# Where VectorE takes its block sums in the first groups of a fused attention and mixer kernel

## The chip, the cores and the metric

The kernel runs on one core of a Trainium2 chip. Its time is the device time of one execution in microseconds (us), and less is better. The core has five engines, each with an instruction queue of its own that it works off in order: TensorE (PE in the profile, its weight loads PEld), VectorE (DVE), ScalarE (ACT), GpSimd (POOL) and SyncE (SP, which here only issues DMAs). They wait for each other through semaphores.

## The reference

```python
xn = _layernorm(x)                                   # 2048 x 512
q  = (xn @ wq).reshape(B, Sq, 32, 128)               # 32 heads of 128
p  = softmax(einsum("bhqd,bhkd->bhqk", q, k_cache) * 128 ** -0.5)
s  = einsum("bhqk,bhkd->bhqd", p, v_cache) ... @ wo  # heads side by side, 4096 -> 512
# g = silu(block_B(xn)): layernorm, w1, gelu, shifts, w2, residual, layernorm, w3, gelu, w4, residual
return x + s * g
```

## The kernel before, in words

Ahead of the attention stands a prologue of some 120 us: layer norms, the mixer block B, and the gates, which go to DRAM. What follows is attention, cut into 128 **units**. Unit u is one head for 512 queries; the order is group g of four heads (8 of them), then query tile qt (4), then head hh in the group (4), so a group has 16 units and units 0 to 15 are group 0 (`units`, line 126). Every unit has eight **slots** p = 0 to 7, and n = 8u + p counts them all. The loop at line 1131 writes out, slot by slot, what each engine is given; nothing reorders it afterwards (`pin` keeps program order). In a slot PE gets two score matmuls (`s_slot`, `ps_s`), two matmuls of probabilities with V for the slot ten slots earlier (`pv_slot`, `ps_o`), and between them small products. ACT takes the exponentials of a slot into a tile `pT` (line 446); two slots share one tile, so a unit has four.

Two kinds of small products lie between those matmuls, and both use a scheme with seven block products where a plain one has eight. The scheme needs sums and differences of blocks, which VectorE makes beforehand.

- **Queries.** From unit 14 on, q for two heads at a time is made from blocks of `xnT` and of `wq`. `x_sum(qt, i)` (lines 355 to 367, run at line 366) makes four sums of each query tile, once for all; number 2 overwrites a block of `xnT` in place, except for tile 3. `w_sum(h, i)` (369 to 376, run at line 375) makes four differences for each pair of heads. `product` issues the matmuls (`ps_q`), and `q_part` (lines 423 to 431) adds them together on VectorE. The last of these, line 431, writes the `qT` that the next unit's score matmuls read. Before unit 14, q comes from plain matmuls, copied out by `q_copy` (line 341).
- **Output projection.** `wo_sum(g, i)` (lines 553 to 563, run at line 562) makes four differences of the group's `wo`; number 2 is made in place in groups 0 to 5, in group 6 in the second buffer of `tw0`. `o_sum` (line 571) makes the sums of the attention output `oT`, each in a single buffer `so0` to `so3`, and `wo_product` issues the matmuls into `ps_wo`. They all use one PSUM tile, tag `xm`, and VectorE's `wo_take` (line 596) adds its halves to the accumulator `sacc` before PE may write there again. The first four token tiles of group 0 use plain matmuls, copied by line 655.

For the softmax denominators VectorE adds the four `pT` tiles of a unit into `acc`: `add_first` (line 452) at slot 4 adds the first two, then the third follows (line 461, or in two halves at line 457: one half by GpSimd from slot 6 of the unit, the other by VectorE early in the next one) and the fourth (line 461). `fold` and `fold_last` (465, 469) halve the result twice. SP transposes it by DMA (`tT`, line 494), VectorE reduces it in the unit after (499, 505), SP sends the reciprocals to DRAM and back to all partitions (`rb`, lines 507 and 511), and the product at line 523 normalizes `ps_o`.

What decides where a sum stands is written out by hand: the list of units in line 1120 for `x_sum` (four for tile 3, then tiles 0, 1 and 2, each at the end of slot 3 of its unit), line 1123 for `w_sum` (slot 4), line 1084 for `wo_sum` (offsets in slots around the group's unit 6, for group 0 unit 10), and `APART` in line 1056 for the units whose third `pT` tile is added in two halves. The tile pool `qt` (line 89) gives `qT` tiles of 1 KB a partition, six in turn.

Of the kernel before, what the change touches and what calls it, by code (L numbers as in the profile page):

```python
# [11 lines left out]
BF16 = mybir.dt.bfloat16  # L12
# [5 lines left out]
def kernel(  # L18
# [16 lines left out]
    P = nc.NUM_PARTITIONS  # L35
# [3 lines left out]
    Sq, D = x2d.shape  # L39
# [11 lines left out]
    HG = 4  # L51
    NG = H // HG
# [11 lines left out]
    def pool(name, bufs=1, space=None, **kw):  # L64
        if space is not None:
            kw["space"] = space
        return tc.tile_pool(name=name, bufs=bufs, **kw)
# [21 lines left out]
    qtp = ent(pool("qt", 6))  # L89
# [11 lines left out]
    pR = right.enter_context(pool("pR", side="right", reuse_waits="tile"))  # L101
# [9 lines left out]
    def mm(out, lhsT, rhs, start, stop, **kw):  # L111
# [9 lines left out]
        out=ident[:], in0=diag[:], scalar1=0.0, scalar2=None, op0=ALU.is_equal))  # L121

    HEAD = 7
    XS = 3 * QT + 1
    TW = (2, 1, 0, 1)
# [3 lines left out]
    NU = len(units)  # L129
# [5 lines left out]
    def at(n, fn):  # L135
        todo[n].append(fn)
# [194 lines left out]
               xnT[:, dc, qt * 512:(qt + 1) * 512], dc == 0, dc == DC - 1)  # L331

    def q_copy(u, eng=None):
        pl, tag = (pR, "qR") if u < HEAD else (qtp, "qT")
        qT = pl.tile([P, 512], BF16, tag=tag, **(dict(bufs=HEAD) if u < HEAD else {}), name="qT")
        src, dst = st[u].pop("psq")[:], qT[:]
        if u in TURN:
            src = src.rearrange("d (r j) -> d j r", j=4)
            dst = dst.rearrange("d (j r) -> d j r", j=4)
        if eng is None:  # L340
            pin(nc.vector.tensor_copy(out=dst, in_=src))
        else:
            pin(nc.scalar.activation(out=dst, in_=src, func=ACT.Identity))
        st[u]["qT"] = qT[:]
# [10 lines left out]
    def x_sum(qt, i):  # L355
        if i == 2 and qt < QT - 1:
            out = x_block(qt, 1, LO)
        else:
            out = pS.tile([P, 2, 256], BF16, tag="xs", bufs=XS, name="xs")[:]
        a, b, op = (  # L360
            (x_block(qt, 1, LO), x_block(qt, 1, HI), ALU.add),
            (xs.get((qt, 0)), x_block(qt, 0, LO), ALU.subtract),
            (x_block(qt, 0, LO), x_block(qt, 1, LO), ALU.subtract),
            (x_block(qt, 0, HI), xs.get((qt, 1)), ALU.subtract),
        )[i]
        pin(nc.vector.tensor_tensor(out=out, in0=a, in1=b, op=op))
        xs[qt, i] = out
# [87 lines left out]
    def add_half(u, eng, part):  # L455
        a, e = st[u]["acc"], st[u]["pT"][2]
        pin(eng.tensor_tensor(out=a[:, part, :], in0=a[:, part, :], in1=e[:, part, :], op=ALU.add))  # L457

    def add_next(u, i):
        a = st[u]["acc"]  # L460
        pin(nc.vector.tensor_tensor(out=a[:], in0=a[:], in1=st[u]["pT"][i][:], op=ALU.add))  # L461
# [91 lines left out]
    def wo_sum(g, i):  # L553
        w = wog[g]
        b11, b12, b21, b22 = (w[:, k, c] for k in (UP, DOWN) for c in (WL, WR))
        if i == 2 and g < NG - 2:
            out = b12
        else:
            j = 0 if i == 2 else i
            out = pS.tile([P, 2, D // 2], BF16, tag=f"tw{j}", bufs=TW[j], name="tw")[:]  # L560
        a, b = ((b12, b11), (b22, tw.get((g, 0))), (b22, b12), (b21, tw.get((g, 1))))[i]
        pin(nc.vector.tensor_tensor(out=out, in0=a, in1=b, op=ALU.subtract))
        tw[g, i] = out
# [46 lines left out]
    wog, sp, tw, so, wo_ps, gin = {}, {}, {}, {}, {}, {}  # L610
# [36 lines left out]
    def pay():  # L647
        while owed:
            y_out(*owed.popleft(), nc.sync)
# [181 lines left out]
    def q_ahead(u):  # L831
        q_mm(u, range(DC), ("xa", "xm")[len(made) % 2])
        q_copy(u, nc.scalar)
        made.append(u)
# [155 lines left out]
    pS = None  # L990
    for h in range(HG):
        load_wo(h)
    for g in range(NG - 1):
        b = (g * QT + QT - 1) * HG
        for hh in range(HG):
            h = (g + 1) * HG + hh
# [56 lines left out]

    FIRST, LAST = 14, NU - 4
    BLOCK = [(g, qt) for g in range(NG - 1) for qt in range(QT)][1:-2]
    APART = range(2 * HG + 1, NU - 3)
    pairs = range(FIRST, LAST + 1, 2)
    q_plan = defaultdict(list)
    steps = defaultdict(list)
# [21 lines left out]
            which[u0 + n].append((o_sum, g, qt, i))  # L1081
    for g in range(NG - 1):
        u0 = ((g * QT + (g == 0)) * HG + 6) * SPU
        for i, n in ((0, -4), (2, -4 if 0 < g < NG - 2 else 4), (1, 4), (3, 12)):
            o_early[u0 + n].append((wo_sum, g, i))
    for i, (qt, u) in enumerate((qt, qt * HG + 5 + j) for qt in range(1, QT) for j in range(2)):
        at(u * SPU + 6, lambda qt=qt, i=i: sa_clear(qt, i % 2))
# [3 lines left out]
    for i, u in enumerate((10, 11, 12, 13, 14, 16, 18, 20)):  # L1091
        n = (LATER + u) * SPU
# [10 lines left out]
    def add_last(u):  # L1103
        if u in APART:
            add_half(u, nc.vector, HI)
        add_next(u, 3)
# [10 lines left out]
        for fn, *args in plan.get(n, ()):  # L1117
            fn(*args)

    for j, u in enumerate((9, 9, 9, 9, 12, 12, 13, 13, 13, 16, 17, 17, 18, 19, 20, 20)):  # L1120
        at(u * SPU + 3, lambda qt=(j // 4 - 1) % QT, i=j % 4: x_sum(qt, i))
    for h in range(2, H, 2):
        for i, u in enumerate((((-4, -3, -3, -3), (-1, -1, 0, 0))[h % HG // 2] if h >= HG else (11,) * 4)):
            o_early[(h // HG * QT * HG + u) * SPU + 4].append((w_sum, h, i))

    for v in range(1, NU):
# [4 lines left out]
    for n in range(UB * SPU):  # L1131
        u, p = divmod(n, SPU)
# [33 lines left out]
        for v, k in ((u + 1, 3), (u + 2, 7)):  # L1166
            if p == k and "psq" in st.get(v, ()) and (k == 3) == (v > FIRST):
                q_copy(v)
# [31 lines left out]
        if p == 6:  # L1200
            add_half(u, nc.gpsimd, LO) if u in APART else add_next(u, 2)
        pay()
# [3 lines left out]
        if pS is None and not held:  # L1206
            right.close()
            pS = right.enter_context(pool("pS", side="right", reuse_waits="tile"))
# [3 lines left out]
    n = UB * SPU  # L1212
# [27 lines left out]
    def pv_to(k):  # L1240
# [29 lines left out]
        out=diag[:], in0=diag[:], scalar1=0.0, scalar2=None, op0=ALU.is_equal))  # L1270
# [98 lines left out]
```

## Time and profile before

| | |
|---|---|
| median of three timed runs | 1224.51 us (1224.1 to 1224.75) |
| the profiled execution: its own time | 1222.83 us |
| its span, first to last instruction | 1221.1 us |
| granted TensorE clock | 1.000 |
| PE, ACT, DVE, POOL busy, share of the span | 99%, 91%, 89%, 24% |

The profile is one execution on the chip. Its page gives busy times, the chain of work that ended last and the costliest groups of instructions. The timeline gives single instructions of one engine: start and duration in us, engine, line of the kernel, operation, output<-inputs with their shapes, and in brackets the idle time of the engine before it with what ended it. Rows of equal instructions that follow each other are merged (x2). Matmuls are pipelined: a matmul of 512 columns is listed with 0.38 us, and two of them with 0.59, but the next one starts 0.216 us after it, so a pair takes 0.43; pairs of 256 columns take 0.22. VectorE's instructions overlap by some hundredths of a microsecond in the same way. The view of windows gives the busy time of each engine in a stretch.

### The profile page before, as it was taken

Reading aid. Unit: us, or ns where it says so; the run is one execution under the profiler, and the core shown is the slowest. Engines: PE = TensorE matmul, PEld = TensorE weight load, DVE = VectorE, ACT = ScalarE, POOL = GpSimd, SP = SyncE. Lnnn points to the kernel's source line nnn. Section 1 sums busy time; section 2 is a strip of 40 time slices with the busy share of each in tenths; the row PEclk is TensorE's granted clock in tenths of the full one; section 3 lists DMA queues with packets and bytes.
Section 4 is the critical chain, followed back from the end, with each engine's and each line's share of the span. In section 5 each row is a group of like instructions: output and inputs, shape, how many; then the busy total and the mean of one; then the engine's idle time right before and its main releaser. Section 6 shows DMA issues by size and latency. Waiting matters only on the chain.

```text
span 1221.1 us, 18821 instructions
## 1 busy us (share of the span) xinstructions
PE 1208.6 (99%) x6534; PEld 673.7 (55%) x6657; DVE 1089.9 (89%) x1931; ACT 1107.6 (91%) x1243; POOL 297.6 (24%) x221
## 2 busy tenths in 40 slices
PE   9999999999999999999999999999999999999998
PEld 6466444555555555555555555555555555555555
DVE  7863778999999999999999899999999999989997
ACT  6345999999999999999999999999999999999996
POOL 5300001233222222222222222222222222223320
PEclk9999999999999999999999999999999999999999
DMA  7662323434343434344344433444433534455552
GB/s 178 169 153 59 56 57 83 96 85 98 75 90 88 99 66 90 85 99 88 70 95 84 103 69 83 92 96 78 87 83 91 100 66 90 87 101 110 124 113 66
DMA packets 248159, 113.07 MB, mean 93 GB/s; under 512 B 195328, under 2 KB 231296, under 8 KB 248064
## 3 DMA queue, kind: packets, MB, share of 16 engines
q1 hardware_dynamic: 244560, 107.21, 40.9%
q0 software_dynamic: 2944, 4.20, 1.5%
q8 instruction: 52, 0.85, 0.3%
q14 instruction: 43, 0.35, 0.2%
q10 hardware_dynamic: 560, 0.46, 0.1%
HBM read 69.60 MB, written 4.45 MB: 61 GB/s over the span
## 4 chain that ended last, share of the span: by engine, by line
PE 92%; DVE 5%; issue 1%; DMA 1%; ACT 1%; SPq 0%; DVEq 0%; POOL 0%; ACTq 0%
PE ps_s L112 39%; PE ps_o L112 35%; PE ps_q L112 8%; PE ps_wo L112 8%; PE ps_m L112 3%; DVE acc L461 1%; DVE acc L452 1%; DVE sacc L596 1%; ACT pT L446 1%; DMA kT<-in_A_k_cache_dram 0%; DVE acc L457 0%; DVE sm L499 0%; DMA tT<-acc 0%; DMA xin<-in_A_x_dram 0%; PE ps_oh L112 0%
## 5 line engine op out<-in xcount | busy, mean ns | idle before, releaser
L446 ACT ACTIVATE pT<-ps_s 128x1024 bf16<-128x1024 f32 x1016 | 1016.6, 1028 | 44.5 <-PE ps_s L112 13.0
L112 PE MATMUL ps_s<-qT,kT 128*128 128x512 bf16 (+1 forms) x2056 | 607.5, 377 | 0.8 <-ACT pT L446 0.4
L112 PE MATMUL ps_o<-pT,vb 128*128 128x512 bf16 x1884 | 568.3, 379 | 4.7
L457 POOL TENSOR_TENSOR acc<-acc,pT 128x1024 bf16<-128x1024 bf16 x116 | 246.8, 2128 | 727.4 <-DVE acc L452 395.6
L112 PEld LDWEIGHTS <-vb 128*128 128x128 bf16 x1984 | 194.0, 98 | 216.5
L112 PEld LDWEIGHTS <-kT 128*128 128x128 bf16 x2064 | 231.0, 113 | 72.4 <-DVE qT L431 1.4
L461 DVE TENSOR_TENSOR acc<-acc,pT 128x2048 bf16<-128x2048 bf16 x138 | 168.9, 1224 | 21.5 <-ACT pT L446 5.5
L452 DVE TENSOR_TENSOR acc<-pT 128x2048 bf16<-128x2048 bf16 x127 | 154.7, 1218 | 11.2 <-ACT pT L446 11.1
L596 DVE TENSOR_TENSOR sacc<-ps_wo,sacc 128x512 f32<-128x512 f32 x200 | 121.6, 608 | 3.4 <-PE ps_wo L112 2.4
L523 DVE TENSOR_TENSOR oT<-ps_o,rb 128x512 bf16<-128x512 f32 x127 | 86.5, 681 | 6.6 <-DMA rb<-dr 5.9
L465 DVE TENSOR_TENSOR acc<-acc 128x1024 bf16<-128x1024 bf16 x127 | 87.3, 687 | 2.4
L499 DVE TENSOR_REDUCE sm<-tT 128x4 f32<-128x512 bf16 x124 | 83.9, 676 | 6.0 <-DMA tT<-acc 5.4
L457 DVE TENSOR_TENSOR acc<-acc,pT 128x1024 bf16<-128x1024 bf16 x116 | 79.6, 686 | 0.0
L112 PEld LDWEIGHTS <-wc 128*128 128x128 bf16 x448 | 43.8, 98 | 52.9
L112 PE MATMUL ps_wo<-wo_h,oT 128*128 128x256 bf16 (+1 forms) x294 | 70.7, 307 | 0.5
L112 PEld LDWEIGHTS <-oT 128*128 128x128 bf16 x428 | 41.6, 98 | 45.6
L112 PEld LDWEIGHTS <-so 128*128 128x128 bf16 x400 | 39.1, 98 | 48.4 <-issue 1.7
L112 PEld LDWEIGHTS <-wq_h 128*128 128x128 bf16 x396 | 38.7, 98 | 46.0
L112 PE MATMUL ps_q<-xnT,wq_h 128*128 128x256 bf16 (+1 forms) x281 | 58.2, 294 | 0.2
L301 ACT ACTIVATE h2T<-ps_s 128x1024 bf16<-128x1024 f32 x28 | 28.7, 1023 | 31.6 <-PE ps_s L112 31.6
L469 DVE TENSOR_TENSOR acc<-acc 128x512 bf16<-128x512 bf16 x127 | 53.4, 420 | 2.4
L112 PEld LDWEIGHTS <-w_sb 128*128 128x128 bf16 x368 | 33.5, 98 | 29.2
(134 smaller groups left out, 924.4 us busy)
## 6 DMA issues: line engine op xcount, KB each, us to landing
rb<-dr SPq DMA_DIRECT2D x127, 256.0 KB, 3.8
vb<-in_A_v_cache_dram SPq DMA_DIRECT2D x62, 256.0 KB, 3.0
wq_h<-in_A_wq_dram SPq DMA_DIRECT2D x32, 128.0 KB, 2.5
wo_h<-in_A_wo_dram SPq DMA_DIRECT2D x32, 128.0 KB, 2.3
w_sb<-in_B_w_dram SPq DMA_DIRECT2D x8, 256.0 KB, 4.6
kT<-in_A_k_cache_dram SPq DMA_TRANSPOSE x128, 2.6
gate<-xall POOLq DMA_DIRECT2D x16, 128.0 KB, 2.3
sacc<-in_A_x_dram POOLq DMA_DIRECT2D x8, 256.0 KB, 4.6
```

Of the source, the lines that this page charges most:

```text
L112: pin(nc.tensor.matmul(out=out, lhsT=lhsT, rhs=rhs, start=start, stop=stop, **kw))
L301: pin(nc.scalar.activation(out=h2[c][:, f], in_=ps[:], func=ACT.Gelu_apprx_tanh))
L446: pin(nc.scalar.activation(out=s["pT"][-1][:, jj:jj + 2, :], in_=sps[:], func=ACT.Exp, scale=SCALE))
L452: pin(nc.vector.tensor_tensor(out=s["acc"][:], in0=s["pT"][0][:], in1=s["pT"][1][:], op=ALU.add))
L457: pin(eng.tensor_tensor(out=a[:, part, :], in0=a[:, part, :], in1=e[:, part, :], op=ALU.add))
L461: pin(nc.vector.tensor_tensor(out=a[:], in0=a[:], in1=st[u]["pT"][i][:], op=ALU.add))
L465: pin(nc.vector.tensor_tensor(out=a[:, 0:2, :], in0=a[:, 0:2, :], in1=a[:, 2:4, :], op=ALU.add))
L469: pin(nc.vector.tensor_tensor(out=a[:, 0, :], in0=a[:, 0, :], in1=a[:, 1, :], op=ALU.add))
L499: pin(nc.vector.tensor_reduce(out=sm[:], in_=s["tT"][:], axis=mybir.AxisListType.X, op=ALU.add))
L523: pin(nc.vector.tensor_tensor(out=to, in0=o, in1=rb, op=ALU.mult))
L596: pin(nc.vector.tensor_tensor(out=out, in0=ps, in1=out, op=ALU.add))
```

## The change

VectorE and GpSimd get the same sums at other places:

- `x_sum`: eight sums move. Tile 3: from unit 9 (four) to units 8, 8, 9, 9. Tile 0: from 12, 12, 13, 13 to 9, 9, 9, 11. Tile 1: from 13, 16 to 11, 13, and its last two stay in 17. Tile 2 stays in 18 to 20.
- `w_sum` of heads 2 and 3: from unit 11 (four) to units 8, 8, 9, 9.
- Unit 8's third `pT` tile is added in two halves, one by GpSimd; before, this began with unit 9.
- `wo_sum` number 2 of group 6: from slot 4 of unit 102 to slot 4 of unit 101, that is eight slots or one unit ahead of where it stood. It now has a tile of the pool `qt` instead of the second buffer of `tw0`. For that the pool's ring of `qT` has five tiles instead of six, and the last unit's `qT` a tile of its own.

The order of instructions on PE, ACT and SP is the same in both kernels.

```diff
     def q_copy(u, eng=None):
-        pl, tag = (pR, "qR") if u < HEAD else (qtp, "qT")
-        qT = pl.tile([P, 512], BF16, tag=tag, **(dict(bufs=HEAD) if u < HEAD else {}), name="qT")
+        pl, tag, n = (pR, "qR", HEAD) if u < HEAD else (qtp, "qT", 5) if u < NU - 1 else (qtp, "qL", 1)
+        qT = pl.tile([P, 512], BF16, tag=tag, bufs=n, name="qT")
...
         if i == 2 and g < NG - 2:
             out = b12
+        elif i == 2:
+            out = qtp.tile([P, 2, D // 2], BF16, tag="qT", bufs=5, name="tw")[:]
         else:
-            j = 0 if i == 2 else i
-            out = pS.tile([P, 2, D // 2], BF16, tag=f"tw{j}", bufs=TW[j], name="tw")[:]
+            out = pS.tile([P, 2, D // 2], BF16, tag=f"tw{i}", bufs=TW[i], name="tw")[:]
...
-    APART = range(2 * HG + 1, NU - 3)
+    APART = range(2 * HG, NU - 3)
...
-        for i, n in ((0, -4), (2, -4 if 0 < g < NG - 2 else 4), (1, 4), (3, 12)):
+        for i, n in ((0, -4), (2, -4 if g else 4), (1, 4), (3, 12)):
...
-    for j, u in enumerate((9, 9, 9, 9, 12, 12, 13, 13, 13, 16, 17, 17, 18, 19, 20, 20)):
+    for j, u in enumerate((8, 8, 9, 9, 9, 9, 9, 11, 11, 13, 17, 17, 18, 19, 20, 20)):
         at(u * SPU + 3, lambda qt=(j // 4 - 1) % QT, i=j % 4: x_sum(qt, i))
     for h in range(2, H, 2):
-        for i, u in enumerate((((-4, -3, -3, -3), (-1, -1, 0, 0))[h % HG // 2] if h >= HG else (11,) * 4)):
+        for i, u in enumerate((((-4, -3, -3, -3), (-1, -1, 0, 0))[h % HG // 2] if h >= HG else (8, 8, 9, 9))):
```

## The prediction

> **What bounds the kernel now.** I read the page first, then the windows, then PE's timeline in the stretches where it idles.
>
> ```profile
> PE 1208.6 (99%) x6534; PEld 673.7 (55%) x6657; DVE 1089.9 (89%) x1931; ACT 1107.6 (91%) x1243; POOL 297.6 (24%) x221
> PE 92%; DVE 5%; issue 1%; DMA 1%; ACT 1%; SPq 0%; DVEq 0%; POOL 0%; ACTq 0%
> ```
>
> PE is busy nearly all of the span, and its instructions stay what they are and in their order. So the change can win only time in which PE stands still. The second row says where to look: VectorE holds 5% of the chain that ended last, in a few stretches where PE came to wait for it. The view of windows, with one row for each stretch, gives the ceiling (PE's busy time is the second figure):
>
> ```profile
> 196.00:270.00 74.00, 72.61 (x368) 38.49 (x374) 70.18 (x130) 68.75 (x75) 21.41 (x12) 1.00 0.45 93
> 980.00:1000.00 20.00, 19.78 (x107) 10.99 (x108) 19.00 (x35) 19.05 (x22) 4.25 (x2) 1.00 0.32 58
> ```
>
> From 196 to 270 us (units 8 to 16, where the moved sums stand) PE idles 1.39 us, and 0.22 from 980 to 1000 (units 101 and 102): 1.6 us in all.
>
> PE's timeline shows the places, and VectorE's the instruction that ended each:
>
> ```profile
> 232.72 0.59 PE L112 MATMUL ps_o<-pT,vb 128*128 128x512 bf16 x2
> 233.78 0.38 PE L112 MATMUL ps_wo<-wo_h,so 128*128 128x256 bf16 x2 [0.47 <-DVE sacc L596]
> ...
> 242.43 0.38 PE L112 MATMUL ps_wo<-tw,oT 128*128 128x256 bf16 x2
> 243.25 0.62 PE L112 MATMUL ps_s<-qT,kT 128*128 128x512 bf16 x2 [0.44 <-ACT pT L446]
> ...
> 267.72 0.59 PE L112 MATMUL ps_o<-pT,vb 128*128 128x512 bf16 x2
> 268.43 0.38 PE L112 MATMUL ps_wo<-wo_h,so 128*128 128x256 bf16 x2
> ```
>
> ```profile
> 233.05 0.68 DVE L596 TENSOR_TENSOR sacc<-ps_wo,sacc 128x512 f32<-128x512 f32 x1
> 242.51 0.68 DVE L431 TENSOR_TENSOR qT<-ps_q,tq 128x512 bf16<-128x512 f32 x1
> 267.70 0.68 DVE L596 TENSOR_TENSOR sacc<-ps_wo,sacc 128x512 f32<-128x512 f32 x1
> ```
>
> A pair of 512 columns takes 0.43 and a pair of 256 takes 0.22, so from start to start PE loses 233.78 - 232.72 - 0.43 = **0.63 us**, 243.25 - 242.43 - 0.22 = **0.60** and 268.43 - 267.72 - 0.43 = **0.28**: 1.51 together (idle time by the records is less, since a record runs 0.16 past the next start). Each time PE starts again 0.05 us after VectorE's row ends (233.73, 243.19, 268.38). The second is put down to ACT, but that exponential ended with it by chance: the matmul reads the `qT` that line 431 had just written. So VectorE is up to 0.6 us late at three points, and each stall carries over: VectorE works without a pause, PE waits for it.
>
> **The change part by part.** Prices and the free room come from VectorE's rows of units 8 to 10, one of PE and one of GpSimd:
>
> ```profile
> 195.72 1.21 DVE L452 TENSOR_TENSOR acc<-pT 128x2048 bf16<-128x2048 bf16 x1
> ...
> 198.15 1.23 DVE L461 TENSOR_TENSOR acc<-acc,pT 128x2048 bf16<-128x2048 bf16 x1 [0.41 <-ACT pT L446]
> 199.29 0.69 DVE L655 COPY sacc<-ps_wo 128x512 f32<-128x512 f32 x1
> ...
> 201.30 1.19 DVE L461 TENSOR_TENSOR acc<-acc,pT 128x2048 bf16<-128x2048 bf16 x1
> ...
> 203.59 0.42 DVE L366 TENSOR_TENSOR xs<-xnT 128x512 bf16<-128x512 bf16 x1
> ...
> 205.06 0.42 DVE L562 TENSOR_TENSOR tw<-wo_h 128x512 bf16<-128x512 bf16 x1
> ...
> 207.75 0.69 DVE L341 CAST qT<-ps_q 128x512 bf16<-128x512 f32 x1 [1.14 <-PE ps_q L112]
> ...
> 210.36 0.66 DVE L457 TENSOR_TENSOR acc<-acc,pT 128x1024 bf16<-128x1024 bf16 x1
> 211.16 1.23 DVE L461 TENSOR_TENSOR acc<-acc,pT 128x2048 bf16<-128x2048 bf16 x1
> ```
>
> ```profile
> 198.62 0.59 PE L112 MATMUL ps_wo<-wo_h,oT 128*128 128x512 bf16 x2
> ```
>
> ```profile
> 1131.19 2.12 POOL L457 TENSOR_TENSOR acc<-acc,pT 128x1024 bf16<-128x1024 bf16 x1 [6.08 <-DVE acc L452]
> ```
>
> ```profile
> 221.31 0.68 DVE L596 TENSOR_TENSOR sacc<-ps_wo,sacc 128x512 f32<-128x512 f32 x1
> ...
> 222.58 0.28 DVE L375 TENSOR_TENSOR wc<-wq_h 128x256 bf16<-128x256 bf16 x1
> ...
> 223.51 1.22 DVE L452 TENSOR_TENSOR acc<-pT 128x2048 bf16<-128x2048 bf16 x1
> ...
> 230.92 0.42 DVE L366 TENSOR_TENSOR xs<-xnT 128x512 bf16<-128x512 bf16 x1
> ...
> 231.71 0.28 DVE L375 TENSOR_TENSOR wc<-wq_h 128x256 bf16<-128x256 bf16 x1
> ```
>
> Four `x_sum`s run from 203.59 to 205.06: 0.37 each. Four `w_sum`s run from 222.58 to 223.51: 0.93, 0.23 each. The two `x_sum`s of unit 12 take 231.71 - 230.92 = 0.79. An addition of a whole `pT` tile takes 199.29 - 198.15 = 1.14, VectorE's half of one 211.16 - 210.36 = 0.80.
>
> *Units 8 and 9* get three `x_sum`s more (1.11) and four `w_sum`s (0.93), and one whole addition becomes a half: + 2.04 - 0.34 = 1.70. Up to the cast at 207.75, which waited for its product, VectorE stood idle 0.41 + 1.14 = 1.55. With everything filled it is 0.15 late there. But now the third copy of line 655 stands ahead of the addition that had waited, and its product ends at 198.62 + 0.59 = 199.21, by when VectorE has caught up: some 0.2 stays idle. I take **0.3 late** after unit 9. Nobody waits for that. The casts wait in any case, and the third copy, whose PSUM tile PE wants next, comes no later than before. GpSimd's half starts when line 452 of unit 8 ends, now at 195.72 + 1.20 + 1.21 = 198.1, and is done by 200.4; VectorE's half follows the third copy by 201.30 - 199.29 = 2.0, as the second addition did, and so comes at about 201.2.
>
> *Unit 11* gets two `x_sum`s ahead of line 596 (0.74) and loses four `w_sum`s behind it: line 596 ends 1.04 later, at 221.31 + 1.04 + 0.68 = 223.03, and the row of unit 11's `acc` comes 0.3 + 0.74 - 0.93 = 0.1 later. PE's next write to that PSUM tile stands at 223.85, so 0.8 are left:
>
> ```profile
> 223.85 0.38 PE L112 MATMUL ps_wo<-wo_h,oT 128*128 128x256 bf16 x2
> ```
>
> *Unit 12* loses 0.79: VectorE is 0.7 **earlier** than before. Line 596 ends at 233.03, PE could go on from 233.15, and the stall of 0.63 goes, with 0.1 to spare. *Unit 13* loses three `x_sum`s and gets one (- 0.74): 1.4 earlier. Line 431 ends at 241.8; PE, itself 0.63 earlier, needs it at 242.02: the stall of 0.60 goes, with 0.2 to spare. *Unit 16* loses one (- 0.37): 1.8 earlier. Line 596 ends at 266.6, PE (1.23 earlier) needs it at 266.92: the stall of 0.28 goes. The transposes and reciprocals between VectorE's own rows go by DMA and move with the rows that feed them. But VectorE does wait for such landings, eight times for the transpose and up to 1.8 us, so margins of 0.1 to 0.3 are the weak point (waits: total, times, longest):
>
> ```profile
> DVE sm L499 <- DMA tT<-acc: 5.4, 8, 1.8
> ```
>
> *Units 101 and 102* lose and gain one `wo_sum`:
>
> ```profile
> 991.69 0.43 DVE L571 TENSOR_TENSOR so<-oT 128x512 bf16<-128x512 bf16 x1 [0.49 <-PE ps_wo L112]
> 992.04 0.42 DVE L562 TENSOR_TENSOR tw<-wo_h 128x512 bf16<-128x512 bf16 x1
> ...
> 992.71 1.22 DVE L452 TENSOR_TENSOR acc<-pT 128x2048 bf16<-128x2048 bf16 x1
> 993.84 0.68 DVE L596 TENSOR_TENSOR sacc<-ps_wo,sacc 128x512 f32<-128x512 f32 x1
> ```
>
> ```profile
> 993.87 0.59 PE L112 MATMUL ps_o<-pT,vb 128*128 128x512 bf16 x2
> 994.58 0.38 PE L112 MATMUL ps_wo<-wo_h,so 128*128 128x256 bf16 x2
> ```
>
> PE loses 994.58 - 993.87 - 0.43 = 0.28, again until line 596 ends (994.52). From 992.04 to 992.71 stand two `wo_sum`s, 0.33 each, and the first goes one unit ahead. There its 0.33 is then swallowed by the wait of 0.49 at 991.69, where VectorE waits for PE to be done with a buffer, and behind that wait VectorE is 0.33 earlier: line 596 ends at 994.19, PE needs it at 994.30, and the 0.28 goes. The new tile costs no wait: its place in the ring was last read in unit 9.
>
> **Sum:** 0.63 + 0.60 + 0.28 + 0.28 = 1.79. The profiled execution's own 1222.83 becomes 1221.04; from the median of 1224.51, 1.68 above it, the same step leads to **1222.7**, a gain of 0.15%. Bounds: nothing won, 1224.5; or PE's other wait for line 431, about 0.4 in group 5, goes too (priced among the rivals).
>
> **The rivals.** *The margins are used up* (1223.4). A DMA that lands 0.2 or 0.3 us later than its mate in this profile leaves VectorE late at 233, 242 or 994. If the first gap stays at half and the last stays, 1.2 are won. For it: margins of 0.1. Against: the DMAs start from rows that are themselves earlier.
>
> *The work is only moved* (1224.2, with the 0.28 at 994 alone). VectorE cannot use the idle time of units 8 and 9, say because the copies there wait longer for their products. Then it is 1.7 late after unit 9 instead of 0.3, the 1.8 that goes until unit 16 only makes up for it, and a stall comes in unit 11 instead, where 0.8 are left. Against it: 1.14 of the 1.55 stand as one wait just in front of a single row.
>
> *GpSimd's additions hold VectorE* (1226.7, slower). A half on GpSimd and an operation of VectorE with two inputs in SBUF do disturb each other:
>
> ```profile
> 1132.96 0.90 DVE L457 TENSOR_TENSOR acc<-acc,pT 128x1024 bf16<-128x1024 bf16 x1
> ```
>
> Line 457 takes 0.90 here against 0.66 at 210.36, where GpSimd had finished: it got going only when GpSimd was done, at 1133.31. If the halves of units 8 and 9, whose times shift, each held VectorE for their full length, it would lose 2 x 2.12 = 4.24, be 4.24 - 1.8 = 2.4 later than before in unit 16, and with 0.28 won at 994 the time would be 1226.7. Slower than before needs a loss of over 1.8 + 0.3 = 2.1. Against it: by the sums above GpSimd ends 0.8 ahead of line 457 in unit 8, and in unit 9, where it follows the cast's start at 208.05, it ends at 210.3, line 457 starting at 210.66; beside it run rows that read PSUM. The Trainium skill, page "SBUF — State Buffer", section "Who interferes with whom", states this as a rule: a VectorE instruction with two SBUF inputs and a GpSimd instruction that reads SBUF exclude each other, and the later one is blocked for the whole instruction. By that rule the half newly given to GpSimd is a danger and not only a relief; the row of 0.90 agrees with it.
>
> *More goes than forecast* (1222.3). PE waits once more for line 431:
>
> ```profile
> 868.18 0.62 PE L112 MATMUL ps_s<-qT,kT 128*128 128x512 bf16 x2 [0.23 <-DVE qT L431]
> ```
>
> That stall is about 0.4 (0.23, and 0.16 that the record before runs past this start). Nothing here is moved, but DMA times differ from run to run.
>
> **How the numbers follow.** Forecast 0.64, margins used up 0.16, work only moved 0.08, held 0.05, more 0.07. About 0.2%, 2.45 us, is what a measurement of this kernel can tell from no change; the forecast of 1.8 lies inside it, and the three runs alone spread over 0.65. Faster by over 0.2% (under 1222.06) takes a part of "more" and of the forecast's scatter: 0.12. Slower by over 0.2% (over 1226.96) needs "held" at its full price and a little more: 0.04. Within: 0.84. The range takes in the first, second and third case and the upper part of "more", and leaves out "held": 1221.8 to 1224.4.
>
> **What would show it.** Right: no gap in PE's timeline near 233, 243, 268 and 994; the cast of unit 9 without idle time before it and some 0.3 us later; line 596 of unit 12 ending ahead of PE's need. Wrong: a gap in units 8 to 11, line 457 of unit 8 or 9 over 0.8 us long, or gaps left at 233 and 994.

## The result, and the profile after

The changed kernel took **1222.41 us** (median of 22 runs, 1220.92 to 1224.74), the kernel before beside it 1224.43 us (22 runs, 1222.9 to 1226.47). The ratio is 0.9984 with a 95% interval of 0.9978 to 0.9991: about 2.0 us faster, between 1.1 and 2.7. The forecast was 1222.7, a gain of 1.8.

But the profiled execution of the changed kernel took 1223.05 us with a span of 1221.3, no less than that of before (1222.83 and 1221.1), where the prediction's sum gave 1221.04. So there are two questions: did the four stalls go, and what stood in their place in this execution?

The page of the changed kernel, engines' busy time and the chain of work that ended last:

```profile
PE 1215.1 (99%) x6657; PEld 673.7 (55%) x6657; DVE 1090.0 (89%) x1931; ACT 1107.5 (91%) x1243; POOL 299.2 (24%) x222
PE 96%; DVE 2%; ACT 1%; DMA 0%; issue 0%; DVEq 0%; ACTq 0%
```

VectorE's busy time is what it was (1090.0 against 1089.9): nothing was taken out, sums only stand elsewhere. Its share of the chain fell from 5% to 2%. (PE's busy time can't be compared between the two pages: one trace holds 6534 matmuls, the other all 6657.)

PE's timeline of the changed kernel at the four places:

```profile
232.84 0.59 PE L112 MATMUL ps_o<-pT,vb 128*128 128x512 bf16 x2
233.27 0.38 PE L112 MATMUL ps_wo<-wo_h,so 128*128 128x256 bf16 x2
...
241.92 0.38 PE L112 MATMUL ps_wo<-tw,oT 128*128 128x256 bf16 x2
242.14 0.59 PE L112 MATMUL ps_s<-qT,kT 128*128 128x512 bf16 x2
...
994.18 0.59 PE L112 MATMUL ps_o<-pT,vb 128*128 128x512 bf16 x2
994.61 0.38 PE L112 MATMUL ps_wo<-wo_h,so 128*128 128x256 bf16 x2
```

From start to start it is 0.43, 0.22 and 0.43, the bare time of the pairs: the gaps of 0.63 at 233, 0.60 at 243 and 0.28 at 994 are gone (the fourth, at 268, too). VectorE's rows that had ended the first two, and the wait that took up the sum of group six (lines from 558 on have one number more than before: 597 was 596):

```profile
232.41 0.68 DVE L597 TENSOR_TENSOR sacc<-ps_wo,sacc 128x512 f32<-128x512 f32 x1
...
241.21 0.68 DVE L431 TENSOR_TENSOR qT<-ps_q,tq 128x512 bf16<-128x512 f32 x1
...
992.00 0.43 DVE L572 TENSOR_TENSOR so<-oT 128x512 bf16<-128x512 bf16 x1 [0.76 <-PE ps_wo L112]
```

In their place stands a gap that before did not have. PE's timeline, then VectorE's:

```profile
258.79 0.38 PE L112 MATMUL ps_wo<-tw,oT 128*128 128x256 bf16 x2
259.85 0.41 PE L112 MATMUL ps_s<-qT,kT 128*128 128x512 bf16 x1 [0.68 <-DVE qT L431]
```

```profile
250.47 0.69 DVE L523 TENSOR_TENSOR oT<-ps_o,rb 128x512 bf16<-128x512 f32 x1 [0.78 <-DMA rb<-dr]
251.51 0.69 DVE L499 TENSOR_REDUCE sm<-tT 128x4 f32<-128x512 bf16 x1 [0.34 <-DMA tT<-acc]
...
259.11 0.68 DVE L431 TENSOR_TENSOR qT<-ps_q,tq 128x512 bf16<-128x512 f32 x1
```

PE loses 0.84 until line 431 has ended (259.79). VectorE works without a pause from 251.51 to there, but it had stood for 0.78 + 0.34 = 1.12 at 250 because two DMAs landed late, the broadcast reciprocals (`rb`) and the transposed sums (`tT`). The same happens twice more: 0.58 at 327, behind a wait of 0.87 for `rb` at 319.25, and 0.61 at 868, behind one of 0.96 for `rb` at 859.79. These three make 2.03, with 0.14 at 1140 they come to 2.17. What was won (0.63 + 0.60 + 0.28 + 0.28, and the 0.40 that before lost at 868) is 2.19.

### The profile page after: what moved, and what is told of

Read it like the earlier page. It is cut to its first block, busy times and chain, and to the rows that moved or that the text cites. A ratio compares the mean times of both kernels' runs of the same rounds, so it can differ in the third digit from the quotient of the medians.

```text
span 1221.3 us, 18941 instructions
## 1 busy us (share of the span) xinstructions
PE 1215.1 (99%) x6657; PEld 673.7 (55%) x6657; DVE 1090.0 (89%) x1931; ACT 1107.5 (91%) x1243; POOL 299.2 (24%) x222
## 4 chain that ended last, share of the span: by engine, by line
PE 96%; DVE 2%; ACT 1%; DMA 0%; issue 0%; DVEq 0%; ACTq 0%
PE ps_s L112 40%; PE ps_o L112 37%; PE ps_q L112 8%; PE ps_wo L112 8%; PE ps_m L112 3%; ACT pT L446 1%; DVE acc L461 0%; PE ps_warm L112 0%; DMA tT<-acc 0%; DVE acc L452 0%; DVE sacc L597 0%; PE ps_oh L112 0%; DVE y L1232 0%; DVE sm L499 0%; DVE acc L457 0%
## 5 line engine op out<-in xcount | busy, mean ns | idle before, releaser
L112 PE MATMUL ps_o<-pT,vb 128*128 128x512 bf16 x1984 | 589.9, 379 | 0.0
```

The costliest lines, as they stand in the source:

```text
L112: pin(nc.tensor.matmul(out=out, lhsT=lhsT, rhs=rhs, start=start, stop=stop, **kw))
```

## Experiments

**Theory:** what counts is where VectorE's work stands. Idle time ahead of unit 9's cast takes up the moved sums, the lateness of units 12 to 16 goes, and the new gaps come from DMAs whose landing differs from one execution to the next. **Rivals:** the new gaps belong to the new order (the work was only moved); the total of VectorE's work counts; the half on GpSimd is what helps, or what hurts.

All runs, with PE's gaps of over 0.12 us, each from start to start less the bare time of the matmuls between. The gaps of the last 10 us, equal in all, are left out:

| kernel | median us | before beside it | ratio, 95% interval | profiled span | gaps of PE |
|---|---|---|---|---|---|
| before | 1224.43 | | | 1221.1 | 0.63 at 233, 0.60 at 243, 0.28 at 268, 0.28 at 994; 0.40 at 868 |
| changed | 1222.41 | 1224.43 | 0.9984, 0.9978 to 0.9991 | 1221.3 | 0.84 at 259, 0.58 at 327, 0.61 at 868, 0.14 at 1140 |
| lists_only | 1221.51 | 1223.74 | 0.9983, 0.9974 to 0.9992 | 1219.2 | 0.28 at 992 |
| half8_only | 1222.87 | 1223.74 | 0.9994, 0.9985 to 1.0002 | 1221.6 | 0.64 at 233, 0.60 at 243, 0.24 at 260, 0.47 at 269, 0.21 at 329, 0.28 at 995 |
| wo6_only | 1223.27 | 1223.74 | 0.9997, 0.9988 to 1.0006 | 1221.0 | 0.64 at 233, 0.60 at 243, 0.49 at 260, 0.46 at 268 |
| after_again | 1220.81 | 1223.74 | 0.9978, 0.9969 to 0.9987 | 1219.5 | 0.16 at 706, 0.13 at 1138 |
| no_half8 | 1221.38 | 1223.30 | 0.9985, 0.9976 to 0.9994 | 1219.6 | 0.17 at 259, 0.43 at 327 |
| add1_in_11 | 1222.68 (one run) | 1223.30 | | 1220.9 | 0.22 at 233; 0.70 at 259, 0.46 at 327, 0.34 at 446, 0.29 at 868 |
| add4_in_11 | 1222.81 | 1223.29 | 0.9997, 0.9988 to 1.0006 | 1220.0 | 0.50 at 224, 0.24 at 226, 0.47 at 233; 0.20 at 867 |
| add4_in_4 | 1221.51 | 1223.29 | 0.9984, 0.9975 to 0.9993 | 1219.8 | 0.41 at 838, 0.46 at 841, 0.26 at 867 |
| pool_beside | 1222.89 | 1223.29 | 1.0002, 0.9993 to 1.0010 | 1220.7 | 0.59 at 218, 0.23 at 224, 0.24 at 227, 0.47 at 234; 0.31 at 1139 |
| so1_later | 1221.30 | 1223.29 | 0.9985, 0.9977 to 0.9994 | 1219.8 | 0.31 at 233, 0.46 at 841 |

Taking the listed gaps from each span leaves 1218.6 to 1219.2 in all twelve. So the gaps account for the spans to within 0.6 us, and a trace can show which part did what even where an interval of 2 us can't.

### The three parts of the change, each alone

**lists_only**: the `x_sum` and `w_sum` lists of the change put into the kernel before.

```diff
-    for j, u in enumerate((9, 9, 9, 9, 12, 12, 13, 13, 13, 16, 17, 17, 18, 19, 20, 20)):
+    for j, u in enumerate((8, 8, 9, 9, 9, 9, 9, 11, 11, 13, 17, 17, 18, 19, 20, 20)):
...
-        ... if h >= HG else (11,) * 4)):
+        ... if h >= HG else (8, 8, 9, 9))):
```

> Only the new lists of x_sum and w_sum; GpSimd's halves begin with unit 9 as before, and the sum of group six stays in unit 102. Theory (place decides: idle time of VectorE in units 8 and 9 takes up the moved sums, and the lateness it saves carries over to unit 16): the whole addition of unit 8 stays on VectorE, so it is 0.34 us later than in the changed kernel at line 596 of unit 12 (about 233.4 instead of 233.09): some 0.28 of the stall of 0.63 at 233 stays, the stalls at 243 and 268 go, the one of 0.28 at 994 stays. 1.2 us are won against before. Rival (DMA landings take the margins, so the gain is chance): no fixed order of the gaps, gain between 0 and 1. Rival (the half on GpSimd is what counts): gain 0, stalls as before.

The lists alone won 2.1 us (1.0 to 3.2 by the ratio's interval), and all three gaps at 233, 243 and 268 are gone. The one of the fourth place stays. PE's timeline of this run at the first and the fourth:

```profile
232.83 0.59 PE L112 MATMUL ps_o<-pT,vb 128*128 128x512 bf16 x2
233.26 0.38 PE L112 MATMUL ps_wo<-wo_h,so 128*128 128x256 bf16 x2
...
991.98 0.59 PE L112 MATMUL ps_o<-pT,vb 128*128 128x512 bf16 x2
992.69 0.38 PE L112 MATMUL ps_wo<-wo_h,so 128*128 128x256 bf16 x2
```

One number of the theory failed: without the half on GpSimd, 0.28 should have stayed at 233. VectorE's rows of unit 8 and the cast of unit 9 in this run, then in the changed kernel, tell why:

```profile
199.10 1.21 DVE L461 TENSOR_TENSOR acc<-acc,pT 128x2048 bf16<-128x2048 bf16 x1
200.22 0.68 DVE L655 COPY sacc<-ps_wo 128x512 f32<-128x512 f32 x1
...
202.22 1.20 DVE L461 TENSOR_TENSOR acc<-acc,pT 128x2048 bf16<-128x2048 bf16 x1
...
208.20 0.69 DVE L341 CAST qT<-ps_q 128x512 bf16<-128x512 f32 x1
```

```profile
199.37 0.69 DVE L656 COPY sacc<-ps_wo 128x512 f32<-128x512 f32 x1 [0.18 <-PE ps_wo L112]
...
201.38 0.66 DVE L457 TENSOR_TENSOR acc<-acc,pT 128x1024 bf16<-128x1024 bf16 x1
202.18 1.23 DVE L461 TENSOR_TENSOR acc<-acc,pT 128x2048 bf16<-128x2048 bf16 x1
...
208.18 0.68 DVE L341 CAST qT<-ps_q 128x512 bf16<-128x512 f32 x1
```

With the whole addition (1.12 from 199.10 to 200.22) VectorE has work until the copy's product is there. With the half it must wait for that product, and then still has its own half to do (0.80). Both reach the fourth addition at the same time, 202.22 and 202.18, and the cast at 208.20 and 208.18: the half saves 0.02 to 0.04, not 0.34. How the gain divides between the list of `x_sum` and that of `w_sum` is not shown: they were only run together.

**half8_only**: the kernel before with `APART = range(2 * HG, NU - 3)`.

> Only the third tile of unit 8 in two halves; lists and group six as before. Theory: the 0.34 us that VectorE saves in unit 8 is lost again in the idle time of 1.14 ahead of the cast of unit 9 (that wait becomes about 1.5), so units 9 to 16 run as before: stalls of 0.6, 0.6 and 0.3 at 233, 243 and 268, 0.28 at 994, time as before within 0.2. Rival (the half on GpSimd counts by itself): the stall at 233 shrinks by 0.34 and the time by 0.3 to 0.6. Rival (GpSimd holds VectorE): line 457 of unit 8 takes over 0.8 us.

The gaps at 233, 243 and 995 stand (0.64, 0.60, 0.28), and the interval of the ratio includes 1. VectorE's timeline of units 8 and 9:

```profile
199.58 0.69 DVE L655 COPY sacc<-ps_wo 128x512 f32<-128x512 f32 x1 [1.50 <-PE ps_wo L112]
...
201.59 0.66 DVE L457 TENSOR_TENSOR acc<-acc,pT 128x1024 bf16<-128x1024 bf16 x1
202.38 1.23 DVE L461 TENSOR_TENSOR acc<-acc,pT 128x2048 bf16<-128x2048 bf16 x1
...
208.07 0.69 DVE L341 CAST qT<-ps_q 128x512 bf16<-128x512 f32 x1 [0.34 <-PE ps_q L112]
```

The saved time is lost, as expected, but at another place and with more lost than saved: the third copy now waits 1.50 for its product, where before the whole addition had filled most of that wait, and the half comes on top afterwards. The fourth addition starts at 202.38 instead of 201.30. This trace begins its score matmuls 0.33 later, so 0.75 of it are real, and the cast's wait shrinks from 1.14 to 0.34 where the theory wanted 1.5. Line 457 took 0.66: GpSimd does not hold it. The gap of 268 is larger here (0.47, at 269), and those of 0.24 at 260 and 0.21 at 329 were not expected: VectorE had waited 0.52 for `tT` at 252.38 and 0.22 at 320.82.

**no_half8**: the changed kernel with `APART` as before, so lists and group six without the half.

> The changed kernel, but unit 8's third tile added whole by VectorE as before: new lists and the sum of group six sooner. The run with the new lists alone had VectorE at the cast of unit 9 at 208.20, the changed kernel at 208.18, since the wait of 0.18 ahead of the third copy takes back most of what the half saves. Theory: no gap at 233, 243, 268 or 994, VectorE's rows of units 9 to 16 within 0.05 of the changed kernel's, time the same within 0.5. Rival (the half is part of the gain): a gap of 0.2 or more at 233, and 0.3 to 0.6 slower than the changed kernel.

No gap at the four places, the cast of unit 9 at 208.24 (the trace begins 0.04 later than the changed kernel's), and the ratio is that of the changed kernel. The half on GpSimd is no part of the gain that the traces or the times can show.

**wo6_only**: the kernel before with `wo_sum` number 2 of group six in unit 101, in a `qT` tile (the edits of `q_copy` and of `wo_sum` itself are those of the change and are left out here).

```diff
-        for i, n in ((0, -4), (2, -4 if 0 < g < NG - 2 else 4), (1, 4), (3, 12)):
+        for i, n in ((0, -4), (2, -4 if g else 4), (1, 4), (3, 12)):
```

> Only the sum of group six one unit sooner, in a tile of the qT ring; lists and halves as before. Theory: the stall of 0.28 at 994 goes, those at 233, 243 and 268 stay (0.6, 0.6, 0.3): 0.28 won, which is below what the timing can tell. Rival (a ring of five qT tiles instead of six holds up line 431 or the cast): a wait on qT that before did not have, in the rows of line 431, and a time 0.3 or more above before.

PE's timeline of this run at 994:

```profile
994.09 0.59 PE L112 MATMUL ps_o<-pT,vb 128*128 128x512 bf16 x2
994.52 0.38 PE L112 MATMUL ps_wo<-wo_h,so 128*128 128x256 bf16 x2
```

From start to start it is 0.43: the gap at 994 is gone, while those at 233 and 243 stand (0.64 and 0.60). The time (0.47 less, interval from 1.5 less to 0.7 more) can't tell 0.28 from nothing, the trace can. Its gap at 268 is 0.46 instead of 0.28, and there is one of 0.49 at 260: behind a wait of 0.76 for `tT` at 252.29. The rival falls: line 431 waits here only for its products (3.9 us in all, nine times; before, 3.5 and eight times), and the cast of line 341 only for its product in unit 9, 1.14 as before. So the ring of five holds up neither.

### The new gaps: place or landing?

**after_again**: the changed kernel, once more.

> The changed kernel once more, for a second trace. Theory: again no gaps at 233, 243, 268 and 994; of the gaps that its first trace had instead (0.84 at 259, 0.58 at 327, 0.61 at 868) those that come from late landings of rb or tT are at other places or of other sizes; time 1.8 to 2.0 below before. Rival (the lateness now shows at fixed new places, 259 and 327, so the work was only moved): the gaps at 259 and 327 come back at the same size, within 0.1.

Neither 259 nor 327 nor 868 has a gap of over 0.12. PE's timeline and VectorE's at the first of them, and PE's at the old place that this execution reaches at 267:

```profile
258.80 0.38 PE L112 MATMUL ps_wo<-tw,oT 128*128 128x256 bf16 x2
259.01 0.62 PE L112 MATMUL ps_s<-qT,kT 128*128 128x512 bf16 x2
...
266.61 0.59 PE L112 MATMUL ps_o<-pT,vb 128*128 128x512 bf16 x2
267.04 0.38 PE L112 MATMUL ps_wo<-wo_h,so 128*128 128x256 bf16 x2
```

```profile
250.67 0.69 DVE L499 TENSOR_REDUCE sm<-tT 128x4 f32<-128x512 bf16 x1 [0.24 <-DMA tT<-acc]
...
258.27 0.68 DVE L431 TENSOR_TENSOR qT<-ps_q,tq 128x512 bf16<-128x512 f32 x1
```

The DMA `rb` that falls into unit 14 was issued at 244.75 in the first trace and at 244.78 in this one. It landed at 250.45 and at 249.72, in lists_only (issued at 244.79) at 248.51. Line 431 follows at 259.11 and 258.27. So the same program in the same order has 2.2 us of gaps or 0.3, by when DMAs land. This execution took 1221.29 us in all; the sum of the prediction had been 1221.04. The rival, work that was only moved, falls: the gaps at 259 and 327 do not come back at their size, and half8_only and wo6_only, which have the old lists, have one at 260 as well (0.24 and 0.49).

### The margin, and whether place decides

**add1_in_11**, **add4_in_11** and **add4_in_4**: the changed kernel with one or four additions of 128x512 more on VectorE, at the end of slot 3 of unit 11 or of unit 4. The edit with four in unit 11:

```diff
+    def extra():
+        outs = [token(False, "dum") for _ in range(2)]
+        for k in range(4):
+            pin(nc.vector.tensor_tensor(
+                out=halves(outs[k % 2][:]), in0=x_block(3, 0, LO), in1=x_block(3, 0, HI), op=ALU.add))
+
+    at(11 * SPU + 3, extra)
```

> The changed kernel with one more VectorE addition of 128x512 (0.34 us, result unused) ahead of line 597 of unit 11. Theory (the margin at 233 is 0.1): no gap in unit 11, where 0.7 to 0.8 are left, and one of 0.2 to 0.25 at 233; none at 243, since PE is late by as much. Rival (VectorE has more room than worked out): no gap.

PE's timeline at 233:

```profile
232.66 0.59 PE L112 MATMUL ps_o<-pT,vb 128*128 128x512 bf16 x2
233.31 0.38 PE L112 MATMUL ps_wo<-wo_h,so 128*128 128x256 bf16 x2
```

One addition (0.33) gives a gap of 0.22 here and none in unit 11: the margin at 233 is 0.11. The prediction had 0.1.

> The changed kernel with work added: four more VectorE additions of 128x512 (some 0.34 us each, 1.36 together, results unused) at the end of slot 3 of unit 11, ahead of line 597 of that unit. Theory (place decides, lateness carries over): PE stalls by some 0.5 us for line 597 of unit 11 near 224, and by unit 12 the sum of the stalls is 1.36 less the margin of 0.1, about 1.25; time 1.2 to 1.3 above the changed kernel. Rival (the total of VectorE's work counts, not its place): 4 x 0.34 of 1090 us busy spread over the span, the same result as for the four additions in unit 4. Rival (VectorE has idle time left after unit 9): no new gap, time as the changed kernel.

VectorE's timeline with the four, then PE's:

```profile
222.11 1.42 DVE L1130 TENSOR_TENSOR dum<-xnT 128x512 bf16<-128x512 bf16 x4
223.46 0.68 DVE L597 TENSOR_TENSOR sacc<-ps_wo,sacc 128x512 f32<-128x512 f32 x1
```

```profile
223.47 0.38 PE L112 MATMUL ps_q<-xnT,wq_h 128*128 128x512 bf16 x1
224.19 0.38 PE L112 MATMUL ps_wo<-wo_h,oT 128*128 128x256 bf16 x2 [0.34 <-DVE sacc L597]
```

The four take 223.46 - 222.11 = 1.35, and PE loses 0.50 + 0.24 + 0.47 = 1.21 of it by unit 12, the first for line 597 of unit 11 as these rows show. In time the kernel is level with before: no gain is left that can be told.

> The changed kernel with work added: the same four VectorE additions (results unused), at the end of slot 3 of unit 4, where VectorE still stands idle between its rows. Theory: no new gap and the time of the changed kernel, within 0.3, though VectorE's busy time is the same as with the four in unit 11. Rival (the total counts): as much slower as with the four in unit 11.

VectorE's timeline of unit 4 with the four additions, and that of the changed kernel without them:

```profile
158.04 1.42 DVE L1130 TENSOR_TENSOR dum<-xnT 128x512 bf16<-128x512 bf16 x4
159.38 1.22 DVE L452 TENSOR_TENSOR acc<-pT 128x2048 bf16<-128x2048 bf16 x1
161.28 1.23 DVE L461 TENSOR_TENSOR acc<-acc,pT 128x2048 bf16<-128x2048 bf16 x1 [0.68 <-ACT pT L446]
```

```profile
159.38 1.23 DVE L452 TENSOR_TENSOR acc<-pT 128x2048 bf16<-128x2048 bf16 x1 [0.99 <-ACT pT L446]
161.54 1.23 DVE L461 TENSOR_TENSOR acc<-acc,pT 128x2048 bf16<-128x2048 bf16 x1 [0.93 <-ACT pT L446]
```

Waits of 0.99 + 0.93 became 0.68, and the ratio is that of the changed kernel: the same work costs nothing here and 1.2 us of PE's time in unit 11. The medians of the two kernels, timed side by side, are 1222.81 - 1221.51 = 1.30 apart, as expected. Its gaps at 838 and 841 stand behind waits of VectorE of 0.65 for `rb` at 832.10 and 1.46 for `tT` at 834.25.

### Does GpSimd hold VectorE?

**pool_beside**: the changed kernel with two GpSimd additions of 128x512 more at slot 7 of unit 9.

```diff
+            pin(nc.gpsimd.tensor_tensor(
+                out=halves(out[:]), in0=x_block(3, 0, LO), in1=x_block(3, 0, HI), op=ALU.add))
```

> The changed kernel with work added: two GpSimd additions of 128x512 (about 1.06 us each by half of the 2.12 of line 457, results unused) at slot 7 of unit 9, so that they run beside VectorE's lines 457 and 461, which have two SBUF inputs. Theory of the slower rival (GpSimd's addition holds VectorE): line 457 or 461 there is 1 to 2 us longer than 0.66 and 1.23, VectorE is as much late from unit 9 on, the stalls at 224, 233 and 243 come back and the time is 0.9 to 2 above the changed kernel. Rival (GpSimd is held instead, or neither): VectorE's two rows keep 0.66 and 1.23, no new gap, GpSimd's two rows longer than 1.06 or not, time as the changed kernel.

GpSimd first had a memset to do, so the two met lines 465 and 469 and not 457 and 461. GpSimd's timeline, then VectorE's:

```profile
210.31 1.17 POOL L548 MEMSET sacc<- 128x1280 f32 x1
211.44 3.78 POOL L1130 TENSOR_TENSOR dum<-xnT 128x512 bf16<-128x512 bf16 x2
```

```profile
210.63 0.66 DVE L457 TENSOR_TENSOR acc<-acc,pT 128x1024 bf16<-128x1024 bf16 x1
211.42 1.22 DVE L461 TENSOR_TENSOR acc<-acc,pT 128x2048 bf16<-128x2048 bf16 x1
212.68 1.52 DVE L465 TENSOR_TENSOR acc<-acc 128x1024 bf16<-128x1024 bf16 x1
214.24 1.26 DVE L469 TENSOR_TENSOR acc<-acc 128x512 bf16<-128x512 bf16 x1
```

Both engines lose. Their instructions end in turn: line 461 at 212.65, GpSimd's first addition at 213.66, line 465 at 214.20, GpSimd's second at 215.22, line 469 at 215.50. Lines 465 and 469 take 1.52 and 1.26 where they take 0.69 and 0.42 elsewhere: 1.67 more. GpSimd's two take 3.78 where two halves of its 2.12 were expected: 1.66 more. Line 461, which had begun 0.02 before GpSimd, kept its 1.22. PE then stalls 0.59 + 0.23 + 0.24 + 0.47 = 1.53 by unit 12, and the kernel is no faster than before. The memset, which reads nothing, ran beside line 457 at its 0.66. The Trainium skill, page "SBUF — State Buffer", section "Who interferes with whom", says that whichever of the two instructions is issued first keeps the shared pair for its whole length while the other is blocked; the rows agree, and they show what that makes of two streams: they take turns, instruction by instruction, and both lose.

### A try at more room for line 431

**so1_later**: the changed kernel with `o_sum` number 1 four slots later, behind line 431.

```diff
-        for i, n, which in (..., (1, 12, o_early), ...):
+        for i, n, which in (..., (1, 16, o_early), ...):
```

> The changed kernel with o_sum number 1 of each odd-unit step four slots later, so behind line 431 instead of ahead of it. The gaps ahead of PE's score matmuls near 259, 327 and 868 in the first trace of the changed kernel were waits for line 431. Theory (these gaps come when rb or tT lands late, and line 431 has a margin of some 0.1 to 0.4): line 431 ends 0.34 earlier in those units, so such a gap is 0.34 smaller or gone; 0 to 0.5 won on average, which the timing can hardly tell. Rival (the sum now comes late for its own product, or line 597 of the next unit is late instead): new gaps ahead of ps_wo, time 0.3 or more above the changed kernel.

No gain over the changed kernel that can be told (0.9985), and a new gap of 0.31 at 233. VectorE's timeline:

```profile
225.48 0.69 DVE L523 TENSOR_TENSOR oT<-ps_o,rb 128x512 bf16<-128x512 f32 x1 [0.34 <-DMA rb<-dr]
...
232.82 0.68 DVE L597 TENSOR_TENSOR sacc<-ps_wo,sacc 128x512 f32<-128x512 f32 x1
```

It is the pattern of half8_only again: the sum had covered the wait for `rb` ahead of line 523 of unit 12. Taken away from there, VectorE waits 0.34, does the sum after it, and line 597 is 0.41 later than in after_again (232.41). Less the margin of 0.11 this is the new gap. For line 431 the move did what it should: in unit 15 it starts 2.27 after line 597 (256.25 to 258.52), in after_again 2.60 (255.67 to 258.27). Whether that closes the gaps at 259, 327 and 868 is not shown: this trace has none there, but after_again has none either.

## Why the prediction was right, point by point

- **Forecast and mechanism: right.** 1222.7 was forecast, 1222.41 measured. The gain is 0.16% (0.09% to 0.22%), where the forecast had 0.15%. The interval leaves out no gain at all, so 22 runs told more than the 0.2% that the prediction gave a measurement. That the two times agree to 0.3 us is in part luck: the 22 runs spread over 3.8 us, and the changed kernel, timed again, won 2.7 (after_again). What doesn't hang on luck are the gaps: all four went, the first three by the lists (lists_only), the last by the sum of group six (wo6_only).
- **Units 8 and 9: right in the sum, with two terms mis-sized that nearly cancel.** The cast of unit 9 starts 208.18 - 207.75 = 0.43 later, 0.12 of which is that this whole trace begins its score matmuls later (115.39 against 115.27): 0.31, forecast 0.3. The copy's idle time is 0.18, forecast 0.2. But the half addition, taken as 0.34 saved of which some 0.2 goes to that idle time, saved 0.02 to 0.04: the whole addition fits where VectorE otherwise waits. And the room was larger than the 1.55 of the idle times, since VectorE's rows overlap: before, it is 1.03 from the second copy to the addition (197.12 to 198.15) and 2.35 from line 452 to the cast (205.40 to 207.75), where lists_only, without a wait, takes 0.55 and 1.14 (198.55 to 199.10, 207.06 to 208.20). That is a room of 0.48 + 1.21 = 1.69, and 2.04 - 1.69 = 0.35 is what lists_only shows (0.45 later, 0.11 of it the later beginning). So 0.3 came out right in part by luck.
- **Units 11 to 16: right.** Line 597 of unit 11 ends at 223.09, forecast 223.03; of unit 12 at 233.09 (233.03), line 431 of unit 13 at 241.89 (241.8), each 0.06 to 0.09 more, which the trace's later beginning (0.12) covers. Unit 16 is read from after_again, which had little waiting there: 266.76 (266.6).
- **Units 101 and 102: right.** Of the 0.33 moved ahead, 0.27 went into the wait of line 572, which grew from 0.49 to 0.76, and the gap of 0.28 closed.
- **"Margins are used up": the margins are small, but landings did not reopen these gaps.** In the traces of the changed kernel (two), lists_only and no_half8, 233, 243 and 268 stayed closed. Late landings bite elsewhere instead, at 259, 327 and 868 in these traces and at 841 in add4_in_4 and so1_later; before has one of these gaps too (0.40 at 868). (By its own terms this rival's time is 1224.5 - 1.2 = 1223.3, not 1223.4.)
- **What the prediction underrated** is the size of that. Away from the four places, "DMA times differ from run to run" was priced as one stall of about 0.4, won or not. In these traces the gaps at other places than the change's four come to 0.3 and 2.2 us in two executions of the changed kernel, and to 0 in lists_only. So the step "1222.83 becomes 1221.04", made against a profiled execution's own time, failed for the first profile of the changed kernel and held for the second (1221.29).
- **"GpSimd's additions hold VectorE": the mechanism is real, its condition did not arise.** pool_beside shows the price (1.67). In the changed kernel GpSimd's half of unit 8 ran from 198.51 to 200.63 and so ended 0.75 ahead of line 457 at 201.38, forecast 0.8. In unit 9 it ended at 210.52, 0.26 ahead of line 457 at 210.78, forecast 210.3 and 210.66. The row of unit 8:

```profile
198.51 2.12 POOL L457 TENSOR_TENSOR acc<-acc,pT 128x1024 bf16<-128x1024 bf16 x1 [2.58 <-DVE acc L452]
```

## What to carry to other kernels

An engine that is 89% busy can still set the time at a few points: look for the stalls of the bounding engine, find the row that ended each, and follow the lateness back to the next idle time; work moved ahead of that idle time is free as far as the idle time takes it up, and the same work behind it is paid but for the margin (1.21 us of 1.35 here, against nothing). Before work is taken away from an engine, see whether it covers a wait: the half addition and the later `o_sum` each saved a third of a microsecond on paper and only uncovered a wait. And where margins are a tenth of a microsecond, one profile is not the kernel: take a second one, and add up the stalls by place, before a new stall is put down to the change.

## What the runs showed of the hardware that was not expected

- The DMA `rb` that is issued in unit 14 (256 KB, at 244.75 to 244.79) took 5.7 and 4.9 us to land in the two traces of the changed kernel and 3.7 in that of lists_only; over all twelve traces it is 3.7 to 5.7. Not all of it is chance: the `rb` that is issued between 1115 and 1118 takes 5.6 to 6.5 in every one of the twelve, where the median of all 127 is 3.6 to 3.9. Why a landing is late stays open: no run here changed the transfers beside it. The Trainium skill, page "DMA: Bandwidth & Descriptors", section "Latency and other measured facts", has 0.2 us for an average access to HBM and 2 us under high load; the spread here, 2.0, is of that size, but no run shows that it comes from there.
- VectorE and GpSimd, each with additions that read SBUF, both slowed: 1.67 and 1.66 us lost on either side over two instructions each.
